# Third pair's increments and scores in one visit, the decay rows beside the spread of a, the second group's two pairs in one block, and no filler products: a Mamba-2 scan with a gated feed-forward block

## Chip, cores and metric

One core of a Trainium2 chip runs the whole kernel in one launch. The metric is the time on the device in microseconds (us), as the median over runs. The core has five engines that are used here: PE (TensorE, with its weight loads shown as PEld), DVE (VectorE), ACT (ScalarE), POOL (GpSimd) and SP, which only issues DMAs. Each engine works through its own queue strictly in the order of the program; between engines, semaphores hold an instruction back until what it needs is there.

## The reference

`batch, heads, seq, head_dim, d_state` are 4, 8, 768, 32, 16. The scan's result is turned to 3072 tokens of 256 values and goes through a feed-forward block with 2048 hidden values. All data are float32, the two weights come as float64.

```python
log_a = np.log(np.clip(a, 1e-06, 1.0))
for c in range(nc):                       # chunks of 32 in the reference
    cum = np.cumsum(la, axis=-1)
    L = np.exp(cum[:, :, :, None] - cum[:, :, None, :]) * causal
    M = np.einsum('bhin,bhjn->bhij', Cc, Bc) * L
    y_intra = np.einsum('bhij,bhjd->bhid', M, xc)
    y_inter = np.einsum('bhin,bhnd->bhid', Cc, state) * np.exp(cum)[:, :, :, None]
    y[:, :, sl] = y_intra + y_inter
    decay_from_j = np.exp(cum[:, :, -1:] - cum)
    Bx = np.einsum('bhjn,bhjd->bhjnd', Bc, xc) * decay_from_j[:, :, :, None, None]
    state = decay_full[:, :, None, None] * state + np.sum(Bx, axis=2)
...
h = x @ w_in                              # x: (3072, 256)
g = h * (1.0 / (1.0 + np.exp(-1.702 * h)))
return g @ w_out
```

## The kernel before, in words

The kernel uses chunks of 128 steps. A *pair* is two neighbouring chunks of all eight heads of one batch (12 pairs, numbered from 0), a *group* is two pairs, 512 tokens (6 groups, numbered from 0). The pairs that the title calls the second group's are pairs 6 and 7: they are turned while group 1, the second, is projected. While the feed-forward part of one group runs on PE, the scan of later groups is woven in between.

The scan of a pair has these steps. `turn_only` transposes B and C on PE into a PSUM tile `tp` (L491) and copies them out on ACT (BT and two CT, L496). `since_start` multiplies C by the decay since the start (CsT, DVE L524). `gain` makes the state's increments A (PE L567, 32-column strips of the array), `keep` turns them into states S on DVE (L582, L589). `score` makes C·B (tile cb, PE L539, 32-row strips), `weigh` multiplies them into the decay matrix L on DVE (L550). `finish` adds the two parts of y on PE (L603, L612) and copies yT out on ACT. `decay` makes the decay matrix of a chunk by a scan on DVE (L347) from rows of `a` that a DMA spread over the partitions, and `ends` scales B by its last column (L392). `clip_rows` and `decay_rows` make the decay since the start of a batch from another copy of `a`.

The opening is different. The decay of the first two pairs comes from logarithms: a cumulative sum on DVE (`cum`, L290), differences on PE (`differ`, L455, on top of a mask that `mask` has put there, L447) and exponentials on ACT (`exps`, L474). Before that, one product of ones (`keep_busy(1)`, L373) and two mask products into a tile that nobody reads (`idle`) run on PE. The weights arrive as two 32-bit words per value and are turned into float32 in ten pieces: `fields` (DVE L157, L160), `clamp` (ACT L168, L169), `rounded` (DVE L173), `join` (DVE L184, L190); `narrow(i)` is `rounded(i)`, `fields(i+1)`, `join(i)`. Pieces 0 to 5 are w_in, 6 to 9 are w_out.

Pair 2 is the third pair. Its decay is made on the chip without a DMA: `fan_all` spreads picked rows of `a` with four products in 32-row strips (L355) into an area of four PSUM banks, and four scans on DVE follow (L382). `since_fanned` makes the rest of batch 0's decay since the start: a spread of six chunks' rows by PE (`rows`, L422), a small one of the starts (`starts`, L436), a copy and a scan on DVE (L441, L442).

Group 0's feed-forward part is plain: `hidden(0, f)` for f from 0 to 15 (PE L654 into a bank `h`, Silu on ACT L657), then `project_all(0)` (PE L766 into two banks `o`), with steps of the scan hung into places of both by `at(in_hidden[0], f, ...)` and `at(in_project[0], f, ...)`. Group 1 has plain hidden products and a projection by seven products of mixed blocks (`product`, PE L823, with operands mixed on DVE by `mix_w`, L791, and `mix_g`, L694 to L696); its steps are H0 to H7 and P0 to P5, with work hung in by `at(after, step, ...)`. Groups 2 to 5 use seven products for the hidden part too (`first`, PE L726 and L736, with `mix_y` making the operands `my`), and the lists of steps in `run` fix the order on PE. In each of them, `ahead` is called two products into the sixth part of the projection: both pairs of a later group are transposed, gained, and kept there, with `mix_y` between.

PSUM: four banks of the pool `ps` (tag "ff") hold, in turn, all of tp, A, h, o, y, X, Y, rows and starts; four more are the area for cb, the spread of `a`, or the accumulators.

Of the kernel before, what the change touches and what calls it, by code (L numbers as in the profile page):

```python
# [16 lines left out]
P = 128  # L17
# [18 lines left out]
def kernel(  # L36
# [41 lines left out]
    NC = S // P  # L78
# [4 lines left out]
    CG = TG // P  # L83
# [79 lines left out]
    def clamp(i):  # L163


        e = power[i]
        z = e.bitcast(FP32)
        nc.scalar.activation(z, e, AF.Relu, scale=-8.0, bias=edge[:, 0:1])  # L168
        nc.scalar.activation(e, z, AF.Relu, scale=-1.0, bias=edge[:, 1:2])  # L169

    def rounded(i):

        nc.vector.scalar_tensor_tensor(out=mantissa[i].bitcast(FP32), in0=bits[i][0],  # L173
                                       scalar=2.0 ** -32, in1=mantissa[i],
                                       op0=ALU.mult, op1=ALU.add)
# [176 lines left out]
    def fan(p, r, ab):  # L352

        rows = slice(32 * r, 32 * r + 32)
        nc.tensor.matmul(out=ab, lhsT=ones[rows], rhs=fans[p][rows].rearrange("p k q i -> p (k q i)"),  # L355
                         start=True, stop=True, tile_position=(32 * r, 0),
                         skip_group_check=True)

    def fan_all(p):

        ab = area(f"ab{p}")
        for r in range(R):
            fan(p, r, ab[:, r])
        for r in range(R):
            decay_heads(p, r, ab[:, r])
        for k in range(2):
            ends(p, k)
# [51 lines left out]
    def fan_rows(t, c0, c1):  # L419

        o = bank(f"rows{c0}")[:, :(c1 - c0) * P]
        nc.tensor.matmul(out=o, lhsT=whose.rearrange("p h n -> p (h n)"),  # L422
                         rhs=t[:32, c0:c1].rearrange("p c s -> p (c s)"), start=True,
                         stop=True, tile_position=(0, 0), skip_group_check=True)
        return o
# [4 lines left out]
        nc.scalar.activation(since[0][:, :CG].rearrange("p c s -> p (c s)"),  # L430
                             fan_rows(cum, 0, CG), AF.Exp)

    def since_fanned():

        t, f = fan_rows(az, CG, NC), bank("starts")[:, :NC - CG]
        nc.tensor.matmul(out=f, lhsT=whose.rearrange("p h n -> p (h n)"),  # L436
                         rhs=starts[1][:32, CG:, 0], start=True, stop=True,
                         tile_position=(0, 0), skip_group_check=True)
        first = ssd.tile([P, NC, P], FP32, tag="first", name="first0", bufs=1)[:, CG:]
        nc.gpsimd.memset(first, 0.0)  # L440
        nc.vector.tensor_copy(first[:, :, 0], f)  # L441
        nc.vector.tensor_tensor_scan(  # L442
            out=since[0][:, CG:].rearrange("p c s -> p (c s)"), data0=t,
            data1=first.rearrange("p c s -> p (c s)"), initial=0.0, op0=ALU.mult, op1=ALU.add)

    def mask(t):
        nc.tensor.matmul(out=t, lhsT=identb, rhs=below.unsqueeze(1).to_broadcast([P, 4, P]),  # L447
                         start=True, stop=False, skip_group_check=True)
# [31 lines left out]
    def bank(name):  # L480
        return ps.tile([P, 4 * P], FP32, tag="ff", name=name)
# [71 lines left out]
    def advance(p):  # L553
        gain(p)
        keep(p)
# [374 lines left out]
    for r in range(2):  # L930
        ab[1, r] = bank(f"ab1_{r}")
        mask(ab[1, r])
    idle = bank("idle")
    for i in range(2):
        mask(idle)
    differ(0, [(r, ab[0, r]) for r in range(R)])
    exps(0, range(R))
    nc.vector.tensor_copy(idents, ident.unsqueeze(1).to_broadcast([P, NH, P]))
# [1 line left out]
    since_exp()  # L940
    fields(0)
    clamp(0)
    score(0, ab0)
    differ(1, [(r, ab[1, r]) for r in range(2)])
    exps(1, range(2))
# [1 line left out]
    ends(0, 0, nc.gpsimd)  # L947
    ends(0, 1, nc.gpsimd)
    weigh(0)
    rounded(0)  # L950
    turn_only(1, ("ACT", "ACT", "ACT"))
    gain(0)
    for r in range(2, R):
# [31 lines left out]
    def at(places, i, *work):  # L985
        places.setdefault(i, []).extend(work)
# [12 lines left out]
    at(in_hidden[0], 8, lambda: pick_a(PG))  # L999
    at(in_hidden[0], 9, lambda: clamp(6))  # L1000
    at(in_hidden[0], 9, lambda: fan_all(PG))
    at(in_hidden[0], 11, since_fanned, lambda: narrow(6))
    at(in_hidden[0], 15, lambda: clamp(7))
    for k in range(2):
        at(in_hidden[0], 5 + k, lambda k=k: spread(CG + 2 + k))
    at(in_hidden[0], 6, lambda: load(PG + 1))
    at(in_project[0], 0, lambda: turn_only(PG), lambda: narrow(7), lambda: since_start(PG))
    at(in_project[0], 1, lambda: advance(PG), lambda: clamp(8), lambda: decay(CG + 2))
    at(in_project[0], 4, lambda: scores(PG), lambda: narrow(8))
    at(in_project[0], 6, lambda: finish(PG), lambda: clamp(9), lambda: decay(CG + 3),  # L1010
       lambda: clip_rows(1), lambda: decay_rows(1))
    at(in_project[0], 7, lambda: turn(PG + 1))
# [9 lines left out]


    after = {}
    n, p = 2 * PG, 3 * PG

    def late(p):
        gain(p)
# [6 lines left out]
       lambda: turn(n + 1))  # L1035
    at(after, "H3", lambda: finish(n), lambda: load(p + 1), lambda: late(n + 1))
    at(after, "H4", lambda: finish(n + 1))
    for k, i in enumerate(("H4", "P0", "P2", "P5")):
        at(after, i, lambda k=k: mix_w(k))
    for j in range(NF // 2):  # L1040
        at(after, f"P{min(j - 1, 5)}" if j else "H4", lambda j=j: mix_g(1, j))
    for k in range(CG):
        at(after, f"P{k}", lambda k=k: decay(3 * CG + k))
        at(after, "H1" if k < 2 else "H3", lambda k=k: spread(3 * CG + k))
    at(after, "P3", lambda: clip_rows(2), lambda: decay_rows(2), lambda: turn(p))
    at(after, "P4", lambda: mix_y(2), lambda: advance(p), lambda: turn(p + 1))
    at(after, "P5", lambda: advance(p + 1))
    assert [b for b in range(NB) if 3 * CG <= b * NC < 4 * CG] == [2]


# [7 lines left out]
    project_all(0, in_project[0])  # L1058
    load(p)
    spread_rows(2)  # L1060
    for step in "H0 H1 H2 H3 H4 P0 H5 P1 H6 P2 H7 P3 P4 P5".split():
        j = int(step[1:])
        if step[0] == "H":
            hidden(1, 2 * j)
            hidden(1, 2 * j + 1)
        else:
            product(1, j)
        for do in after.get(step, []):
            do()
# [14 lines left out]

    def seven(g, j):
        return [(g, j, (i,)) for i in ORDER]

    for g in range(2, NG):
        n, p = (g + 1) * PG, (g + 2) * PG
        more, most = g + 1 < NG, g + 2 < NG  # L1090
        chunks = list(range((g + 2) * CG, (g + 3) * CG)) if most else []
        rows = [b for b in range(NB) if most and (g + 2) * CG <= b * NC < (g + 3) * CG]
        if most:
            load(p)
            for c in chunks[:2]:
                spread(c)
            for b in rows:
                spread_rows(b)
        run(g, "0.1 P P 0.6 P P 0.7 P 0.5 P 0.2 P 0.D", seven(g - 1, 6))
        run(g, "1.1 0.S P 0.4 P P 1.6 P 0.3 0.T M P P 1.7 P 1.5 1.2 1.D C", seven(g - 1, 7),  # L1100
            M=lambda: mix_g(g, 0), C=lambda: combine(g - 1))
        def along():
            for r in rows:
                clip_rows(r)
                decay_rows(r)

        def refill():
            if most:
                load(p + 1)
                for c in chunks[2:]:  # L1110
                    spread(c)

        if more:

            run(g, "2.1 1.S 1.4 1.3 2.6 2.5 2.2 2.7 1.T s1 2.D 2.S w1 give 2.4 3.1 2.3 3.5 2.T 3.6 "
                "s2 w2 y1 refill 3.7 3.2 3.D along 4.1 P P 3.4 P 3.S 4.6 P 3.3 4.5 3.T M1 P P y2 4.7 P 4.2 4.D M2",
                seven(g, 0), s1=lambda: score(n), w1=lambda: weigh(n), give=lambda: give(g - 1),
                s2=lambda: score(n + 1), w2=lambda: weigh(n + 1), y1=lambda: finish(n),
                refill=refill, along=along, y2=lambda: finish(n + 1), M1=lambda: mix_g(g, 1),
                M2=lambda: mix_g(g, 2))  # L1120
            if most:
                decay(chunks[0])
        else:
            run(g, "2.1 1.S 1.4 1.3 2.6 2.5 2.2 2.7 1.T 2.D 3.1 2.S 2.4 3.5 3.6 2.3 3.2 3.7 2.T 3.D M",
                M=lambda: mix_g(g, 1))
        for j in range(5 if more else 4, NF // 2):
            h = "{1}.1 {0}.S P {0}.4 P {1}.6 P {0}.3 P {1}.7 {0}.T P {1}.5 P {1}.2 P {1}.D M".format(j - 1, j)
            run(g, h, seven(g, j - 4), M=lambda: mix_g(g, j - 2))
            if most:
                decay(chunks[j - 4])  # L1130
        k = NF // 2 - 1
        run(g, f"P {k}.S P {k}.4 P P {k}.3 {k}.T P P P", seven(g, 4))
        if not more:
            give(g - 1)
            for j in range(k - 1, k + 1):
                mix_g(g, j)
            break
        mix_g(g, 6)

        def ahead():  # L1140
            if most:
                for k in (p, p + 1):
                    turn_only(k)
                for k in (p, p + 1):
                    gain(k)
                for k in (p, p + 1):
                    since_start(k)
            mix_y(g + 1)
            if most:
                for k in (p, p + 1):  # L1150
                    keep(k)

        run(g, "P P A P P P P P", seven(g, 5), A=ahead)
        mix_g(g, 7)
    end(NG - 1, 5)

# [31 lines left out]
```

## Time and profile before

| what | us |
|---|---|
| median of 5 runs (375.55 to 376.22) | 375.86 |
| the profiled execution's own time | 375.86 |
| its span, first to last instruction | 374.1 |
| PE busy | 367.0 |
| PE weight loads busy | 284.9 |
| DVE busy | 267.4 |
| ACT busy | 152.2 |
| POOL busy | 10.6 |

The time of a run is 1.76 us more than the span: what lies around the instructions. DVE is busy for 71% of the span on the average, but that average hides two parts: in the stretch from 24 to 88 us, DVE has work nearly throughout (15.57 of 16 us and 45.27 of 48 us), while from 143 us on it has 141.88 of 231 us. PE is busy nearly throughout from 24 us to the end.

A row of the timeline has the start, the length, the engine, the source line, the operation, what is written and read, the shape (stationary rows * columns, then moving), and how many records were merged. One float32 product is two records of PE. In brackets: how long the engine had been idle and what ended that.

### The profile page before, as it was taken

To read this page: it belongs to the slowest core of one execution; us is meant where nothing else is said; L and a number is where in the kernel's file an instruction comes from. 1 tells how busy PE (TensorE), PEld (TensorE's weight loads), DVE (VectorE), ACT (ScalarE), POOL (GpSimd) and SP (SyncE) were. 2 spreads that over 40 slices of the span, in tenths; PEclk is the share of its full clock that TensorE was granted. 3 is DMA by queue.
4 is the path that set the end of the run, shared out by engine and by line. 5 is a ranking of instruction groups with operands and counts; after the bars stand their busy time and mean duration, and the time that the engine had idled before them with its cause. 6 is when DMAs were issued, how large, how long until landed. Compare 5 with 4: busy or idle time off the path is not lost.

```text
span 374.1 us, 5767 instructions
## 1 busy us (share of the span) xinstructions
PE 367.0 (98%) x2280; PEld 284.9 (76%) x2280; DVE 267.4 (71%) x439; ACT 152.2 (41%) x337; POOL 10.6 (3%) x34
## 2 busy tenths in 40 slices
PE   8999999999999999999999999999999999999995
PEld 4674467886457588788888878888878888888884
DVE  4899999999879966777887665888574355544443
ACT  4678562402321132553423554333454331554330
POOL 4200000100000010000000000000000000000000
PEclk9999999999999999999999999999999999999999
DMA  9998699715856110086300063000010000000011
GB/s 151 229 328 143 212 238 144 212 42 102 194 131 124 58 42 0 2 156 126 112 3 1 0 123 105 0 2 0 0 58 2 0 3 1 0 2 0 0 58 56
DMA packets 85794, 29.56 MB, mean 79 GB/s; under 512 B 75720, under 2 KB 79240, under 8 KB 85768
## 3 DMA queue, kind: packets, MB, share of 16 engines
q1 hardware_dynamic: 83320, 28.81, 33.0%
q10 hardware_dynamic: 2448, 0.39, 0.6%
q8 instruction: 18, 0.29, 0.3%
q14 instruction: 8, 0.07, 0.1%
HBM read 25.95 MB, written 3.24 MB: 78 GB/s over the span
## 4 chain that ended last, share of the span: by engine, by line
PE 94%; DVE 3%; ACT 1%; issue 1%; DVEq 0%; ACTq 0%
PE acc L823 32%; PE X L726 15%; PE h L654 13%; PE Y L736 11%; PE o L766 8%; PE cb L539 3%; PE y L612 3%; PE y L603 2%; PE h L668 1%; PE tp L491 1%; DVE L L550 1%; PE oT L857 1%; PE A L567 1%; PE ab L447 1%; PE busy L373 1%
## 5 line engine op out<-in xcount | busy, mean ns | idle before, releaser
L823 PE MATMUL acc<-mg,mw 128*128 128x256 f32 x240 | 65.3, 379 | 0.0
L731 ACT ACTIVATE ac<-X 128x256 f32<-128x256 f32 x64 | 24.5, 383 | 68.9 <-PE X L726 68.9
L823 PEld LDWEIGHTS acc<-mg,mw 128*128 128x128 f32 x240 | 45.6, 190 | 6.2
L654 PE MATMUL h<-yT,w_in 128*128 128x512 f32 x112 | 50.0, 595 | 0.0
L840 DVE TENSOR_TENSOR gT<-Y,ac 128x512 f32<-128x512 f32 x32 | 22.1, 691 | 38.8 <-PE Y L736 35.7
L703 ACT ACTIVATE gT<-gT 128x512 f32<-128x512 f32 x64 | 33.3, 520 | 28.5 <-DVE gT L840 28.5
L823 PE MATMUL acc<-gT,w_out 128*128 128x256 f32 x160 | 43.8, 380 | 0.0
L347 DVE TENSOR_TENSOR_SCAN L<-a,idents 128x1024 f32<-128x1024 f32 x18 | 41.1, 2282 | 0.0
L726 PE MATMUL X<-my,mi 128*128 128x256 f32 x128 | 38.7, 384 | 0.0
L654 PEld LDWEIGHTS h<-yT,w_in 128*128 128x128 f32 x112 | 20.8, 190 | 23.4 <-issue 22.4
L823 PEld LDWEIGHTS acc<-gT,w_out 128*128 128x128 f32 x160 | 30.1, 190 | 5.4 <-issue 1.4
L840 DVE TENSOR_TENSOR gT<-Y,b 128x256 f32<-128x256 f32 x32 | 13.5, 421 | 28.0 <-PE Y L736 27.7
L657 ACT ACTIVATE gT<-h 128x512 f32<-128x512 f32 x28 | 16.6, 595 | 39.6 <-PE h L654 39.5
L550 DVE TENSOR_TENSOR L<-L,cb 128x2048 f32<-128x2048 f32 (+1 forms) x12 | 25.3, 2107 | 5.7 <-PE cb L539 5.5
L766 PE MATMUL o<-w_out,gT 128*128 128x256 f32 x128 | 29.3, 383 | 0.0
L694 DVE TENSOR_TENSOR mg<-gT 128x512 f32<-128x512 f32 x40 | 27.3, 683 | 1.9 <-ACT gT L703 1.9
L726 PEld LDWEIGHTS X<-my,mi 128*128 128x128 f32 x128 | 23.8, 190 | 4.2 <-issue 1.2
L766 PEld LDWEIGHTS o<-w_out,gT 128*128 128x128 f32 x128 | 23.8, 190 | 4.1 <-issue 0.7
L823 PE MATMUL acc<-gT,mw 128*128 128x256 f32 (+1 forms) x86 | 24.0, 368 | 0.4 <-DVE c L840 0.4
L823 PE MATMUL acc<-mg,w_out 128*128 128x256 f32 x80 | 23.5, 379 | 0.0
L634 ACT ACTIVATE yT<-y 128x256 f32<-128x256 f32 x22 | 7.2, 381 | 35.8 <-PE y L612 35.5
L736 PE MATMUL Y<-yT,mi 128*128 128x256 f32 x64 | 19.5, 386 | 0.0
(145 smaller groups left out, 541.3 us busy)
## 6 DMA issues: line engine op xcount, KB each, us to landing
a<-scratch SPq DMA_DIRECT2D x18, 512.0 KB, 5.1
bits<-in_moe_w_out_dram SPq DMA_DIRECT2D x4, 1024.0 KB, 7.5
x<-in_x_dram SPq DMA_DIRECT2D x24, 128.0 KB, 3.2
out_dram<-ob SPq DMA_DIRECT2D x11, 256.0 KB, 2.4
bits<-in_moe_w_in_dram SPq DMA_DIRECT2D x4, 512.0 KB, 5.5
bits<-in_moe_w_in_dram SPq DMA_DIRECT2D x2, 1024.0 KB, 8.9
b<-in_B_dram SPq DMA_DIRECT2D x24, 64.0 KB, 3.7
c<-in_C_dram SPq DMA_DIRECT2D x22, 64.0 KB, 2.5
```

The costliest lines, as they stand in the source:

```text
L347: nc.vector.tensor_tensor_scan(out=Ls[p][:, k].rearrange("p r q i -> p (r q i)"), data0=ra[n], data1=idents.rearrange("p h i -> p (h i)"), ...
L550: nc.vector.tensor_tensor(out=Lv[:, k], in0=Lv[:, k], in1=cb.rearrange("p r k e -> p k r e")[:, k], op=ALU.mult)
L654: nc.tensor.matmul(out=h, lhsT=w_in[:, k, f * P:(f + 1) * P], rhs=yT[g][:, k], start=(k == 0), stop=(k == NK - 1))
L657: nc.scalar.activation(gT[g, j][:, i], h, AF.Silu, scale=GELU_SCALE)
L694: nc.vector.tensor_tensor(out=t[:, 0:2], in0=B[:, :, 1], in1=B[:, 0], op=ALU.subtract)
L703: nc.scalar.activation(o, i, AF.Silu, scale=GELU_SCALE)
L726: nc.tensor.matmul(out=s["X"], lhsT=lhsT, rhs=rhs, start=i == "1", stop=i == "4", skip_group_check=True)
L731: nc.scalar.activation(copy, s["X"], AF.Copy)
L736: nc.tensor.matmul(out=o, lhsT=lhsT, rhs=rhs, start=s.pop("new", False), stop=i != "5", skip_group_check=True)
L766: nc.tensor.matmul(out=o[k // 2][:, k % 2], lhsT=gT[g, f // 2][:, f % 2, k * P:(k + 1) * P], rhs=w_out[:, f], start=(f == 0 and k % 2 == 0 ...
L823: nc.tensor.matmul(out=acc[g][0][i][:, cols], lhsT=lhsT, rhs=rhs[:, cols], start=(j == 0 and i in (0, 2, 5, 6)), stop=(j == NF // 2 - 1), ...
L840: nc.vector.tensor_tensor(out=o, in0=v, in1=w, op=ALU.add)
```

## The change

Five edits, four of which move work on PE:

- The two filler products into `idle` are gone, and with them that PSUM bank.
- `rounded(0)` on DVE goes from behind `weigh(0)` to before `score(0)`.
- `since_fanned` is cut in two: its two products (`rows`, `starts`) go into a new function `fan_since`, called inside `fan_all` directly behind the four products of the spread, two hidden tiles earlier on PE. Its DVE part is hung in behind `fan_all`; the order on DVE stays as it was.
- Pair 2's `gain` goes from step 1 of group 0's projection to step 2, and its `score` from step 4 to step 2, directly behind `gain`. `weigh` stays at step 4.
- Pairs 6 and 7 were turned, gained and kept one after the other at P3, P4 and P5 of group 1, with `mix_y(2)` at P4. Now P5 becomes a `run` with `ahead` two products in, as in the later groups; `ahead` has moved out of the loop to be called there too. `mix_w(3)` and `mix_g(1, 6)` go from P5 to P4, and `mix_g(1, 7)` goes behind the last product of P5.

The order of instructions on ACT, POOL and SP is the same in both kernels; no DMA is moved.

```diff
@@ fan_all
         for r in range(R):
             fan(p, r, ab[:, r])
+        fan_since()
         for r in range(R):
             decay_heads(p, r, ab[:, r])
...
-    def since_fanned():
-
-        t, f = fan_rows(az, CG, NC), bank("starts")[:, :NC - CG]
+    def fan_since():
+        t = fanned["rows"] = fan_rows(az, CG, NC)
+        f = fanned["starts"] = bank("starts")[:, :NC - CG]
         nc.tensor.matmul(out=f, lhsT=whose.rearrange("p h n -> p (h n)"),
                          rhs=starts[1][:32, CG:, 0], start=True, stop=True,
                          tile_position=(0, 0), skip_group_check=True)
+
+    fanned = {}
+
+    def since_fanned():
+
+        t, f = fanned["rows"], fanned["starts"]
         first = ssd.tile([P, NC, P], FP32, tag="first", name="first0", bufs=1)[:, CG:]
...
-    idle = bank("idle")
-    for i in range(2):
-        mask(idle)
     differ(0, [(r, ab[0, r]) for r in range(R)])
...
     clamp(0)
+    rounded(0)
     score(0, ab0)
...
     weigh(0)
-    rounded(0)
     turn_only(1, ("ACT", "ACT", "ACT"))
...
-    at(in_hidden[0], 11, since_fanned, lambda: narrow(6))
+    at(in_hidden[0], 9, since_fanned)
+    at(in_hidden[0], 11, lambda: narrow(6))
...
-    at(in_project[0], 1, lambda: advance(PG), lambda: clamp(8), lambda: decay(CG + 2))
-    at(in_project[0], 4, lambda: scores(PG), lambda: narrow(8))
+    at(in_project[0], 2, lambda: gain(PG), lambda: score(PG), lambda: keep(PG),
+       lambda: clamp(8), lambda: decay(CG + 2))
+    at(in_project[0], 4, lambda: weigh(PG), lambda: narrow(8))
...
-    for k, i in enumerate(("H4", "P0", "P2", "P5")):
+    for k, i in enumerate(("H4", "P0", "P2", "P4")):
         at(after, i, lambda k=k: mix_w(k))
     for j in range(NF // 2):
-        at(after, f"P{min(j - 1, 5)}" if j else "H4", lambda j=j: mix_g(1, j))
+        if j < 7:
+            at(after, f"P{min(j - 1, 4)}" if j else "H4", lambda j=j: mix_g(1, j))
...
-    at(after, "P3", lambda: clip_rows(2), lambda: decay_rows(2), lambda: turn(p))
-    at(after, "P4", lambda: mix_y(2), lambda: advance(p), lambda: turn(p + 1))
-    at(after, "P5", lambda: advance(p + 1))
+    at(after, "P3", lambda: clip_rows(2), lambda: decay_rows(2))
...
-    for step in "H0 H1 H2 H3 H4 P0 H5 P1 H6 P2 H7 P3 P4 P5".split():
+    for step in "H0 H1 H2 H3 H4 P0 H5 P1 H6 P2 H7 P3 P4".split():
...
+    def ahead(g, p=None):
+
+        pairs = (p, p + 1) if p else ()
+        for k in pairs:
+            turn_only(k)
+        for k in pairs:
+            gain(k)
+        for k in pairs:
+            since_start(k)
+        mix_y(g)
+        for k in pairs:
+            keep(k)
+
+    run(1, "P P A P P P P P", seven(1, 5), A=lambda: ahead(2, p))
+    mix_g(1, 7)
```

More of the change, by code (lines that the diff above doesn't have):

```diff
@@ L1006 @@
     at(in_hidden[0], 6, lambda: load(PG + 1))
+    n, p = 2 * PG, 3 * PG
     at(in_project[0], 0, lambda: turn_only(PG), lambda: narrow(7), lambda: since_start(PG))
-    at(in_project[0], 1, lambda: advance(PG), lambda: clamp(8), lambda: decay(CG + 2))
-    at(in_project[0], 4, lambda: scores(PG), lambda: narrow(8))
+    at(in_project[0], 2, lambda: gain(PG), lambda: score(PG), lambda: keep(PG),
+       lambda: clamp(8), lambda: decay(CG + 2))
+    at(in_project[0], 4, lambda: weigh(PG), lambda: narrow(8))
     at(in_project[0], 6, lambda: finish(PG), lambda: clamp(9), lambda: decay(CG + 3),
@@ L1024 @@
     after = {}
-    n, p = 2 * PG, 3 * PG
     def late(p):
@@ L1138 @@
         mix_g(g, 6)
[L1140 to L1153, printed above, removed]
+        run(g, "P P A P P P P P", seven(g, 5), A=lambda: ahead(g + 1, p if most else None))
         mix_g(g, 7)
```

## The prediction

> **What bounds the kernel now.** I read the page's busy shares first, then PE's waits, then PE's timeline around each edit, with DVE's and ACT's beside it.
>
> ```profile
> PE 367.0 (98%) x2280; PEld 284.9 (76%) x2280; DVE 267.4 (71%) x439; ACT 152.2 (41%) x337; POOL 10.6 (3%) x34
> ...
> PE ab L539 <- ACT L L474: 0.5, 1, 0.5
> PE h L668 <- DVE w_in L190: 0.4, 1, 0.4
> PE acc L823 <- DVE c L840: 0.4, 1, 0.4
> ```
>
> PE is the bound: 98% busy, and the listed waits come to 1.3 us after its start. So only three things can move the time: PE work taken away, a new wait of PE, and the opening, where PE still waits for others. The first of these is not products here but switches. Take the merged rows of the timeline:
>
> ```profile
> 39.45 1.14 PE L355 MATMUL ab<-X,ones 32*128 32x512 f32 x8
> 40.52 3.70 PE L654 MATMUL h<-yT,w_in 128*128 128x512 f32 x8
> 44.15 0.69 PE L422 MATMUL rows<-az,whose 32*128 32x256 f32 x2
> 44.68 0.28 PE L436 MATMUL starts<-starts,whose 32*128 32x2 f32 x2
> 44.89 7.13 PE L654 MATMUL h<-yT,w_in 128*128 128x512 f32 x16
> ...
> 87.20 3.60 PE L654 MATMUL h<-yT,w_in 128*128 128x512 f32 x8
> ```
>
> Eight h records between whole-array neighbours take 3.43 (from 87.20 to the transposes at 90.63), eight between two visits to strips 3.63 (40.52 to 44.15). So leaving the whole array costs 0.10 and coming back 0.10, whatever is done there. Three edits join visits. No edit moves a DMA, and the order on ACT, POOL and SP stays, so only the queues of PE and DVE are argued below. The same switch is seen at the other two places:
>
> ```profile
> 54.12 0.32 PE L567 MATMUL A<-x,Be 128*32 128x64 f32 x8
> 54.37 5.45 PE L766 MATMUL o<-w_out,gT 128*128 128x256 f32 x24
> 59.74 1.15 PE L539 MATMUL cb<-CT,BT 32*128 32x256 f32 x16
> ...
> 73.67 0.43 PE L567 MATMUL A<-x,Be 128*32 128x64 f32 x16
> 74.03 1.15 PE L539 MATMUL cb<-CT,BT 32*128 32x256 f32 x16
> ...
> 138.07 0.43 PE L567 MATMUL A<-x,Be 128*32 128x64 f32 x16
> 138.43 0.44 PE L491 MATMUL tp<-ident,b 128*128 128x128 f32 x2
> ...
> 142.04 0.43 PE L567 MATMUL A<-x,Be 128*32 128x64 f32 x16
> ...
> 196.84 0.54 PE L567 MATMUL A<-x,Be 128*32 128x64 f32 x24
> ```
>
> **Decay rows with the spread.** Now: 0.10 to leave h, 0.74 in strips (44.15 to 44.89), 0.11 to come back (the 16 h records take 6.97 against 2 x 3.43): 0.95. Directly behind the spread, in 32-row strips already and with the way back paid anyway: two rows records at 0.215 (the later pitch at 44.47 to 44.68) and 0.03 for starts: 0.46. Gain 0.49; if the rows still paid a switch of their own at both ends, 0.28. I take 0.45, as the strips are the same. Something is given back: rows and starts now hold two of the four "ff" banks through three hidden tiles, and h_13 takes the bank of starts, so it waits for the copy L441, with all of PE behind it. The DVE order is unchanged, so L441 still ends at 46.28; PE comes to h_13 at 40.52 + 0.46 + twelve h records at 0.429 + 0.10 = 46.23. Wait 0.05 to 0.10. h_14 waits for the scan L442, done at 47.01, a microsecond before PE. Next, group 0's first projection product needs w_out from L190, which ends at 51.72; PE comes at 52.29 - 0.40 = 51.89. Cover 0.17, so the whole edit cannot bring over 0.57. Sum: 0.40 (0.20 to 0.49).
>
> **Third pair's increments and scores.** Now: leave 0.10, A 0.25 (54.12 to 54.37), back and out again 0.19 (24 o records take 5.37 against 24 x 0.216 = 5.18), cb 1.08 (59.74 to 60.82), back 0.10: 1.72. Pair 3 does both in one visit: 0.10 + 0.36 + 1.08 + 0.10 = 1.64 with twice the A records; eight more A records cost 0.36 - 0.25 = 0.11, so 1.53. Gain 0.19 (bounds 0.10 and 0.29, one switch or three). The score comes 16 o records (3.46) earlier. It needs CT, which ACT ends at 55.88 (row at 55.05, 0.83), or 55.48 after the first gain, as ACT's work there follows the last Silu and so PE. PE reaches the score at 51.89 + 16 x 0.216 + 0.10 + 0.25 = 55.70. Cover 0.2; behind it all of PE would wait. DVE's order stays: CsT, `keep`, the scan L347, then `weigh`, which waited 0.1 for the score and no longer does; it now ends near 62.7, and `finish`, at 64.47 - 0.59 = 63.88, still comes over 1 us later.
>
> **Second group's pairs in one block.** Now, from 134.51: transposes 0.44, back and forth with 0.10 (14 acc records take 3.12, elsewhere 3.02), A 0.36, transposes 0.49, 0.10, A 0.36, back 0.11: 1.96. As in the later groups (195.88 to 196.84 for eight transposes with the way out, A 0.48 for 24 records and 0.11 for eight more, back 0.10): 1.65. Gain 0.31 (0.20 to 0.35). What could wait: DVE does `mix_w(3)`, `mix_g(1, 5)`, `mix_g(1, 6)` from 134.0 on, 4.5 us by their rows (1.46 + 2 x 1.52), done at 138.5. PE begins the transposes at 134.51 + 3.02 (P4) + 0.86 (two products) = 138.40. ACT's copies of one pair now end 1.75 after its transposes begin (136.26), the second pair's follow 1.05 later, at 141.2; then CsT 0.4 on DVE and two of `my`'s operations, 0.69 and 0.43: usable from 142.7. PE asks for it after transposes and A (1.65), five products (2.16), X (0.43) and two products (0.86), at 143.5. In group 2 the same step is asked 5.0 us after the transposes began, and there PE didn't wait; here 5.1 us. If it slipped, X and all that follows would wait by as much. The four "ff" banks are all held for a moment (two tp, two A); X needs the first tp's, free at 140.5, and comes at 142.1. `mix_g(1, 7)` ends about 146.6, before DVE's next step at 147.1.
>
> **No fillers, and `rounded(0)`.**
>
> ```profile
> 5.20 1.49 DVE L290 TENSOR_TENSOR_SCAN cum<-carry,cum 128x256 f32<-128x256 f32 x2 [0.48 <-ACT cum L285]
> ...
> 5.63 0.87 PE L447 MATMUL idle<-below,identb 128*128 128x512 bf16 x2
> 6.43 1.15 PE L455 MATMUL ab<-cum,pick 32*128 32x256 f32 x16
> ```
>
> The first of the two scans has told PE at 6.12 that `differ` may go; the second filler is in the way, and `differ` starts at 6.43. Other starts come 0.05 after their release (the score at 10.63, released 10.58), so without fillers 6.17: gain 0.26. From here to 24 us a chain passes it on: `differ`, the exponentials (8.51), score, the second `differ`, its exponentials (17.00), `ends` on DVE at 18.12, w_in at 23.65, h at 23.80. `rounded(0)`, 0.68, falls into DVE's 0.90 of idle time before `weigh(0)` at 11.99 and buys nothing itself, as `ends` waits for ACT; it gives DVE 0.6 of slack there. Without that idle time it would cost 0.68 on the path to w_in.
>
> But the array is slow at first: the two records of its first product (L373, float32, 512 columns) start 1.02 apart, h records of the same size later 0.429; the masks start 0.427 apart (3.50 to 6.06), two of the same at 14.38 only 0.28. The granted clock's first record is at 6.18, 4.97 us after PE's first product, all of them busy. Without fillers PE is busy for 4.43 us, then idle for 0.53. No row shows what that does. If the clock still comes at 6.18, gain 0.26. If not, `differ` runs at half speed: its eight steps of 0.216 cost 1.73 more, less 0.26 for the earlier start: 1.47 lost, or more if it lasts. I take the 0.26: of the 4.97 us that now precede the grant 4.43 stay busy, 89%, and the idle 0.55 at 10.08 did not slow what followed.
>
> The Trainium skill, "TensorE: Matmul & The Clock Gate", section "Why this matters for your kernels", asks to keep TensorE busy for 4 us or more without a break, and its Part 1 has a free-running window of 3413 ns. The rule's 4 us are met before the gap, the window that would end at 6.18 is not full; by the latter reading the clock would come at 9.59 and the sum would be a gain of 0.90 less 1.47, a loss of 0.57.
>
> **Sum.** 0.40 + 0.19 + 0.31 + 0.26 = 1.16 on a span of 374.1. The profiled execution's own time equals the median, 375.86, so 374.70. The likeliest case's own range, from the bounds: 374.4 to 375.3 (lowest 0.49 + 0.29 + 0.35 + 0.31 = 1.44, highest 0.20 + 0.10 + 0.20 + 0.10 = 0.60, with 0.10 where the clock comes a little later and 0.31 where `differ` also closes the gap to 6.12; rounded).
>
> **Rivals.** (1) *The clock comes late.* One mechanism, the gap at 5.64. For it: the fillers end just where `differ` starts. Against it: the 89%. If the clock comes as long after 6.17 as it now comes after 1.21, at 11.14, only `differ` is hit (the later products wait for ACT): 375.86 - 0.90 + 1.47 = 376.4. If it stays away until the increments end at 14.45, the score, the second `differ` and the transposes (3.8 us of PE) nearly double, some 2.5 more: 379. Slower than before once it costs over 0.90.
> (2) *DVE keeps the pace.* DVE is busy nearly throughout from 24 to 88 us, and the cover at 51.72 is 0.17, at CT 0.2. If DVE or ACT falls behind by 0.3 to 0.5, the first two gains go into a wait: 375.86 - 0.57 = 375.3. Against it: DVE and PE both move with the opening.
> (3) *The block comes too early for DVE.* `my` late by 0.5 more than its cover of 0.8 would leave 375.2; by 1.3 more, nothing is left of the change, 376.0. Against it: group 2's rows.
>
> **How the numbers follow.** Forecast 0.55, (1) 0.27, (2) 0.12, (3) 0.06. About 0.2%, 0.75 us, is what a measurement of this kernel can tell from no change. Faster than 375.11: 0.53 of the forecast, 0.04 of (2), 0.01 of (3): 0.58. Within: 0.02, 0.08, 0.05 of these and 0.09 of (1): 0.24. Slower than 376.61: 0.18 of (1), its longer forms. Range 374.3 to 376.6: the forecast, (2), (3), the short form of (1), and 0.1 below for the spread of a median.
>
> **What would show it.** After: `differ` at 6.17 with eight steps of 0.216, w_in at 23.4; rows directly behind the spread with h_13's wait below 0.1; no PE wait at the score or at `my`; one visit each. Steps of 0.43 in `differ` would prove (1). I'd be wrong by more if a wait appears in a later group, where nothing was changed.

## The result, and the profile after

The changed kernel takes 374.94 us in the median of 21 runs (374.73 to 375.30), beside 375.72 for the kernel before in the same comparison (41 runs, 375.53 to 376.38). The ratio is 0.9977, with the 95% interval 0.9971 to 0.9983: the median is 0.78 us lower. Its profiled execution took 375.30 us, the slowest of the 21, with a span of 373.6; that of before took 375.86 with 374.1. So the profiled pair differs by 0.56 only. That it shows 0.2 less than the medians do is itself a result, as will be seen.

The busy shares of the changed kernel, and PE's waits (what waited, for whom, us in total, times, the longest):

```profile
PE 366.1 (98%) x2278; PEld 285.2 (76%) x2278; DVE 267.8 (72%) x439; ACT 152.1 (41%) x337; POOL 10.8 (3%) x34
...
PE ab L546 <- ACT L L481: 0.6, 1, 0.6
PE h L675 <- DVE w_in L190: 0.4, 1, 0.4
PE acc L830 <- DVE c L847: 0.4, 1, 0.4
PE ab L462 <- DVE cum L290: 0.3, 1, 0.3
```

PE is busy for 0.9 less and remains the bound. The three waits of before, for L, w_in and c, are still there. One is new: `differ` (L462) now stands and waits for the cumulative sum, where the fillers were. Neither the third pair's score nor `my` is in the list.

PE's timeline of the changed kernel, at the rows, at the third pair, at the second group's block:

```profile
39.60 1.14 PE L355 MATMUL ab<-X,ones 32*128 32x512 f32 x8
40.56 0.59 PE L423 MATMUL rows<-az,whose 32*128 32x256 f32 x2
41.00 0.27 PE L437 MATMUL starts<-starts,whose 32*128 32x2 f32 x2
41.20 10.72 PE L661 MATMUL h<-yT,w_in 128*128 128x512 f32 x24
...
55.74 0.32 PE L574 MATMUL A<-x,Be 128*32 128x64 f32 x8
55.99 1.15 PE L546 MATMUL cb<-CT,BT 32*128 32x256 f32 x16
57.07 6.31 PE L773 MATMUL o<-w_out,gT 128*128 128x256 f32 x28
...
138.10 0.38 PE L498 MATMUL tp<-ident,b 128*128 128x128 f32 x2
138.32 0.38 PE L498 MATMUL tp<-ident,c 128*128 128x128 f32 x2
138.54 0.38 PE L498 MATMUL tp<-ident,b 128*128 128x128 f32 x2
138.76 0.38 PE L498 MATMUL tp<-ident,c 128*128 128x128 f32 x2
139.07 0.65 PE L574 MATMUL A<-x,Be 128*32 128x64 f32 x32
139.65 0.70 PE L830 MATMUL acc<-gT,mw 128*128 128x256 f32 x2
```

Each of the three places has one visit to the strips now: the rows start 0.41 behind the start of the spread's last record, with no return in between; A and cb follow each other; the eight transposes are followed by all 32 records of A. But the 24 records of h behind the rows last 10.72, where 23 steps of 0.429, one length of 0.59 and 0.10 for coming back make 10.56: 0.16 has gone somewhere. And the opening is slower than before:

```profile
3.11 2.73 PE L454 MATMUL ab<-below,identb 128*128 128x512 bf16 x6
6.10 1.63 PE L462 MATMUL ab<-cum,pick 32*128 32x256 f32 x16 [0.26 <-DVE cum L290]
7.56 1.04 PE L462 MATMUL ab<-minus,cum 32*128 32x256 f32 x16
```

`differ` does start 0.33 earlier than before (6.43), yet its first half takes 1.63 instead of 1.15, so the second half begins at 7.56, later than before's 7.40. A trace also holds records of the clock that was granted to TensorE, each with its start and length. The first of them, at full clock, starts at 7.12 here and at 6.18 before. Ahead of 7.12 the steps of `differ` last 0.59 and 0.43, behind it 0.22.

Comparing the starts of the same PE records in the two traces, step by step, gives: opening +0.16; rows -0.41, then +0.15 given back among the hidden records before 47.1; third pair -0.20; second group's block -0.29; nothing at any later group. The sum is -0.59, beside -0.56 in the spans. `my`, which the prediction feared for, is ready in time: the two of its operations on DVE that the prediction names end at 142.37, and PE's first product with it starts at 143.21.

### The profile page after: what moved, and what is told of

It reads as the page before. It is cut to its first block, busy times and chain, and to the rows that moved or that the text cites. A ratio compares the mean times of both kernels' runs of the same rounds, so it can differ in the third digit from the quotient of the medians.

```text
span 373.6 us, 5764 instructions
## 1 busy us (share of the span) xinstructions
PE 366.1 (98%) x2278; PEld 285.2 (76%) x2278; DVE 267.8 (72%) x439; ACT 152.1 (41%) x337; POOL 10.8 (3%) x34
## 4 chain that ended last, share of the span: by engine, by line
PE 94%; DVE 2%; ACT 1%; DMA 1%; issue 0%; ACTq 0%; DVEq 0%
PE acc L830 32%; PE X L733 15%; PE h L661 13%; PE Y L743 11%; PE o L773 8%; PE cb L546 3%; PE y L619 3%; PE y L610 2%; PE ab L462 2%; PE h L675 1%; PE tp L498 1%; PE oT L864 1%; ACT L L481 1%; PE A L574 1%; DMA az<-in_a_dram 1%; DVE L L557 1%
## 5 line engine op out<-in xcount | busy, mean ns | idle before, releaser
L743 PE MATMUL Y<-yT,mi 128*128 128x256 f32 x64 | 19.5, 386 | 0.0
```

Source lines behind the costliest of these rows:

```text
L743: nc.tensor.matmul(out=o, lhsT=lhsT, rhs=rhs, start=s.pop("new", False), stop=i != "5", skip_group_check=True)
```

## The experiments

All times below are medians with the number of runs, and ratios are against runs of the kernel before, made beside them on the same chip. The recorded ratio is not the quotient of the two medians, so both are given. The kernels were measured in four groups, each with the kernel before beside it: the changed kernel (after) alone; the four with one part each (no_fill to block_only); early_copy with after_fill2, after_nobusy and after_late_rounded; after_again with early_copy_again and early_both. The mean of the kernel before was 375.82, 375.95, 375.93 and 375.82 in these groups, so a difference of 0.1 between kernels of two groups says nothing until each is set against its own before. Since the opening turned out to differ from execution to execution, the table also gives, from each profiled execution, the first record of the granted clock, the start of `differ`, the start of the first product of `h` from `y` ("h", near 19.5; the opening is what lies before it), and the time from there to the start of PE's last product. This last column has nothing of the opening in it: over the five executions that differ from the changed kernel in the opening at most it stays within 349.40 to 349.41, while h lies anywhere from 19.23 to 20.41.

| kernel | clock granted | differ | h | h to last product | lowest | median |
|---|---|---|---|---|---|---|
| before | 6.18 | 6.43 | 19.55 | 350.14 | 375.53 | 375.72 |
| no_fill | 4.41 | 6.09 | 19.21 | 350.15 | 375.55 | 375.74 |
| rows_only | 4.12 | 6.09 | 19.21 | 349.89 | 375.27 | 375.29 |
| third_only | 6.21 | 6.45 | 19.56 | 349.95 | 375.35 | 375.57 |
| block_only | 4.67 | 6.19 | 19.30 | 349.86 | 375.25 | 375.46 |
| after | 7.12 | 6.10 | 19.71 | 349.40 | 374.73 | 374.94 |
| after_again | 4.09 | 6.11 | 19.23 | 349.41 | 374.80 | 374.83 |
| after_fill2 | 6.90 | 6.62 | 19.86 | 349.41 | 374.81 | 375.43 |
| after_nobusy | 8.56 | 6.09 | 20.41 | 349.41 | 374.80 | 375.48 |
| after_late_rounded | 6.29 | 6.22 | 19.35 | 349.41 | 374.82 | 375.01 |
| early_copy | 6.76 | 6.09 | 19.52 | 349.29 | 374.66 | 374.72 |
| early_copy_again | 4.73 | 6.11 | 19.23 | 349.30 | 374.71 | 374.85 |
| early_both | 6.88 | 6.11 | 19.59 | 349.30 | 374.66 | 374.76 |

**One part at a time.** Four kernels have one edit each on top of the kernel before.

no_fill:

```diff
-    idle = bank("idle")
-    for i in range(2):
-        mask(idle)
```

> The kernel before without the two filler products of the opening, nothing else. Theory: differ can start some 0.26 to 0.33 us earlier, but the grant of the full clock comes at its own moment, which differs from execution to execution; what the first products gain is lost again when they run at half speed up to the grant. Median 0.00 to 0.26 below before, some 0.12 (375.6 beside 375.72); the profile's first product of differ near 6.1 and w_in between 23.4 and 23.9, depending on where the grant falls. Rival 1 (the fillers cost their own time and nothing else): 0.26 below, 375.46. Rival 2 (the fillers are what keeps the array busy enough for the grant, so the clock comes later without them): level to 0.6 above, 375.7 to 376.3.

Measured: 375.74 (12 runs) beside 375.83 (35), ratio 0.9992 (0.9984 to 1.0001). That is 0.09 in the median and 0.15 in the mean, near the theory's average of 0.12, but the ratio's centre fits rival 1's 0.26 (a ratio of 0.9993) better, and the interval holds no gain at all as well. So the times do not decide between the two. What speaks against rival 1 are the lowest times, which are level (375.55 and 375.54): in some executions the fillers cost nothing. Rival 2's loss of up to 0.6 would be a ratio of up to 1.0016, and all of it above 0.04 lies outside the interval. In the profiled execution the clock was granted at 4.41, before the place where the fillers were.

rows_only:

```diff
             fan(p, r, ab[:, r])
+        fan_since()
...
-    at(in_hidden[0], 11, since_fanned, lambda: narrow(6))
+    at(in_hidden[0], 9, since_fanned)
+    at(in_hidden[0], 11, lambda: narrow(6))
```

> The kernel before with the decay rows taken together with the spread of a, nothing else. Theory: 0.41 gross at the rows, and 0.15 given back at h_13, which waits 0.05 for the first copy of the starts and loses 0.10 more on restarting: 0.26 below before, 375.46. Rival 1 (what was predicted: a wait below 0.1 and no more): 0.35 to 0.40 below, 375.35. Rival 2 (VectorE sets the pace behind it, so the shift is lost at the first scores): within 0.10 of before.

Measured: 375.29 (12 runs) beside 375.83, ratio 0.9983 (0.9975 to 0.9992). The median fits rival 1 or more. The trace says otherwise: h to the last product is 0.25 shorter, and the lowest time is 0.27 below before's, as the theory has it. The rest of the median's 0.54 must then lie in the opening, which the edit does not touch; seven of the twelve runs lie between 375.27 and 375.29, and the profiled one of these (375.27) had its clock early, at 4.12.

third_only:

```diff
-    at(in_project[0], 1, lambda: advance(PG), lambda: clamp(8), lambda: decay(CG + 2))
-    at(in_project[0], 4, lambda: scores(PG), lambda: narrow(8))
+    at(in_project[0], 2, lambda: gain(PG), lambda: score(PG), lambda: keep(PG),
+       lambda: clamp(8), lambda: decay(CG + 2))
+    at(in_project[0], 4, lambda: weigh(PG), lambda: narrow(8))
```

> The kernel before with the third pair's increment and score products issued together, nothing else. Theory: one change of product shape is saved both ways, 0.20 below before, 375.52, with no wait of TensorE at that score. Rival (the score now waits for its masked operands, or the increment's later end delays VectorE): 0.00 to 0.10 below, and the wait is to be seen at the score.

Measured: 375.57 (11 runs) beside 375.83, ratio 0.9991 (0.9983 to 1.0000); lowest 0.19 lower, h to the last product 0.19 shorter. The interval holds the theory's 0.20 and the rival's 0.00 to 0.10; the trace decides. PE's timeline of third_only has no gap in front of the scores:

```profile
52.30 3.62 PE L766 MATMUL o<-w_out,gT 128*128 128x256 f32 x16
55.85 0.32 PE L567 MATMUL A<-x,Be 128*32 128x64 f32 x8
56.10 1.15 PE L539 MATMUL cb<-CT,BT 32*128 32x256 f32 x16
57.18 7.17 PE L766 MATMUL o<-w_out,gT 128*128 128x256 f32 x32
```

block_only is the second group's part alone (the lists of `at` and `run` for group 1, and `ahead` outside the loop):

```diff
-    at(after, "P3", lambda: clip_rows(2), lambda: decay_rows(2), lambda: turn(p))
-    at(after, "P4", lambda: mix_y(2), lambda: advance(p), lambda: turn(p + 1))
-    at(after, "P5", lambda: advance(p + 1))
+    at(after, "P3", lambda: clip_rows(2), lambda: decay_rows(2))
...
+    run(1, "P P A P P P P P", seven(1, 5), A=lambda: ahead(2, p))
+    mix_g(1, 7)
```

> The kernel before with the second group's two pairs turned in one block, nothing else. Theory: 0.29 to 0.31 below before, 375.42, with no wait at my. Rival (my's copy comes too late once the block is moved, since the rows' earlier end is not there to help): a wait of 0.1 to 0.8 at my or at the second pair's output, 0.2 below to 0.5 above before.

Measured: 375.46 (12 runs) beside 375.83, ratio 0.9986 (0.9977 to 0.9994); lowest 0.29 lower, h to the last product 0.28 shorter. PE's list of waits shows nothing at `my`.

The three parts together: 0.25 + 0.19 + 0.28 = 0.72 from h to the last product, where the changed kernel has 350.14 - 349.40 = 0.74. They add up, so none of the three hides another.

**The opening.** PE's timeline of after_again, which is the changed kernel itself in another execution, and of rows_only, which still has the fillers:

```profile
3.12 1.92 PE L454 MATMUL ab<-below,identb 128*128 128x512 bf16 x6
6.11 1.15 PE L462 MATMUL ab<-cum,pick 32*128 32x256 f32 x16 [1.07 <-DVE cum L290]
7.08 1.05 PE L462 MATMUL ab<-minus,cum 32*128 32x256 f32 x16
```

```profile
3.11 1.94 PE L454 MATMUL ab<-below,identb 128*128 128x512 bf16 x6
4.89 0.59 PE L454 MATMUL idle<-below,identb 128*128 128x512 bf16 x2
6.09 1.15 PE L462 MATMUL ab<-cum,pick 32*128 32x256 f32 x16 [0.61 <-DVE cum L290]
```

The six masks take 1.92 and 1.94 here and 2.73 in the profiled executions of before and after: the clock came during them, at 4.09 and 4.12. Then the fillers are through at 5.5, `differ` waits for the cumulative sum all the same, and starts at 6.11 without them and at 6.09 with them. So in these executions the fillers cost nothing. What they cost where the clock comes late, after_fill2 shows:

```diff
+    idle = bank("idle")
+    for i in range(2):
+        mask(idle)
     differ(0, [(r, ab[0, r]) for r in range(R)])
```

> The changed kernel with the two filler products put back, nothing else. Theory: executions in which the clock is granted early (below 4.7) cost nothing more, those in which it comes late cost 0.17 to 0.33; lowest time within 0.05 of the changed kernel's 374.73, mean some 0.12 above its 374.95. Rival 1 (the fillers cost their own time always): 0.26 above in lowest and mean. Rival 2 (the fillers keep the array busy for the grant): level or faster, by up to 0.4.

Measured: 375.43 (11 runs) beside 375.90 (33), ratio 0.9981 (0.9973 to 0.9990); lowest 374.81. The lowest time speaks for the theory against rival 1, at 0.08 rather than within 0.05. The mean is 0.29 above that of the changed kernel, but 0.10 of this stands between the two groups' means of the kernel before; the other 0.19, with standard errors of 0.09 and 0.04 for the two kernels, lies between the theory's 0.12 and rival 1's 0.26 and tells neither from the other. Its profiled execution is a late one:

```profile
3.11 2.73 PE L454 MATMUL ab<-below,identb 128*128 128x512 bf16 x6
5.63 1.06 PE L454 MATMUL idle<-below,identb 128*128 128x512 bf16 x2
6.62 1.25 PE L462 MATMUL ab<-cum,pick 32*128 32x256 f32 x16
```

With the clock at 6.90, the fillers run at half speed to the end and `differ` starts at 6.62, not 6.43; h begins at 19.86, while early_both, without fillers and with the clock at 6.88, has it at 19.59. In this one pair of late executions, then, the fillers cost 0.27. That is about half of the 0.51 by which `differ` starts later, as it should be if the part of `differ` that could have run in that time would have run at half speed. In early executions they cost nothing that can be seen: rows_only with fillers has h at 19.21, no_fill and after_again without them at 19.21 and 19.23. In block_only, with fillers, h comes at 19.30, but there too `differ` waited for the cumulative sum, which itself came late. How often an early or a late clock occurs is not settled by these few executions.

What sets the clock's moment? after_nobusy leaves out the product of ones, two records on PE (its bank is still taken, so that the other tiles come in the same banks):

```diff
-    keep_busy(1)
+    bank("busy")
```

> The changed kernel without the warming products that run from 1.2 to 3.1, so that TensorE's first product is the one at 3.1; the output stays the same. Theory (the full clock is granted at the end of a window of 3.413 of which the array was busy for most, with a phase that nobody sets): the first grant lies between 6 and 9.5 instead of between 4 and 7.2, so the median is 0.5 to 1.2 above the changed kernel, and the executions spread more widely. Rival (the grant comes at a fixed delay from the first product, some 3 to 4): a spread no wider than now, all executions slower by about 1.0. Third case (the phase alone decides, whatever the array did): level with the changed kernel.

Measured: 375.48 (11 runs, 374.80 to 376.17) beside 375.90, ratio 0.9988 (0.9979 to 0.9996). The spread is 1.37 instead of 0.57, the clock came at 8.56 in the profiled execution, and the fastest execution is as fast as the changed kernel. The median is 0.54 above the changed kernel's, which is at the theory's lower edge; against the kernel before of each group it is 0.36. In kind this is the theory. A fixed delay from the first product would not have widened the spread, and the changed kernel itself speaks against one: its clock came 2.88 us after PE's first product in after_again and 5.92 after it in after. Against the third case, that the phase alone decides, stands that the clock did not come one window earlier, at 8.56 - 3.41 = 5.15, though PE had been at work for the last 2.04 of the 3.41 us ahead of it (60%); the intervals of the two ratios overlap a little, so the times alone do not rule it out. PE in that execution:

```profile
3.11 2.72 PE L454 MATMUL ab<-below,identb 128*128 128x512 bf16 x6 [3.11 <-POOL below L273]
6.09 2.09 PE L462 MATMUL ab<-cum,pick 32*128 32x256 f32 x16 [0.27 <-DVE cum L290]
```

The first half of `differ` starts at about the same moment as in after_again (6.11) and takes 2.09 instead of 1.15.

after_late_rounded puts `rounded(0)` back:

```diff
-    rounded(0)
     score(0, ab0)
...
     weigh(0)
+    rounded(0)
```

> The changed kernel with the rounding of the first pair's operands back behind the first weigh, nothing else. Theory (its move was hidden in VectorE's idle time ahead of the weigh, and nothing waits for it there): within 0.06 of the changed kernel in mean and in lowest time. Rival (the move brought part of the gain that is put down to the other parts): slower by 0.1 to 0.3.

Measured: 375.01 (9 runs) beside 375.90, ratio 0.9978 (0.9968 to 0.9987): 0.07 above the changed kernel in the median, 0.10 in the mean (standard errors 0.06 and 0.035), 0.09 in the lowest. Taken so, that is above the theory's 0.06 and at the edge of the rival's 0.1. But the kernel before of this group also has a mean 0.10 higher; against their own before the two means are level (0.87 below it each), as are the ratios, 0.9978 and 0.9977. Its trace has h at 19.35 with `differ` at 6.22 (here the cumulative sum came later), so 13.13 between them; after_again has 13.12. So nothing of the move is to be seen on the path.

**The stall behind the rows.** early_copy is the changed kernel with the copy of the starts ahead of the four scans of the spread on DVE:

```diff
         fan_since()
+        first_since()
         for r in range(R):
             decay_heads(p, r, ab[:, r])
...
-    def since_fanned():
-
-        t, f = fanned["rows"], fanned["starts"]
+    def first_since():
         first = ssd.tile([P, NC, P], FP32, tag="first", name="first0", bufs=1)[:, CG:]
+        fanned["first"] = first
         nc.gpsimd.memset(first, 0.0)
-        nc.vector.tensor_copy(first[:, :, 0], f)
+        nc.vector.tensor_copy(first[:, :, 0], fanned["starts"])
+
+    def since_fanned():
+
+        t, first = fanned["rows"], fanned["first"]
         nc.vector.tensor_tensor_scan(
```

> The changed kernel with the first copy of the starts issued ahead of the four scans of the spread instead of behind them, so that the bank of the starts is free before h_13 asks for it. Theory (the 0.15 given back at h_13 is that wait of 0.05 and a restart of 0.10, both gone with the wait): no wait of TensorE at h_13, 0.15 below the changed kernel, 374.8 beside 374.95. Rival 1 (the 0.10 behind the wait belongs to h after the rows, whatever waits): 0.05 below. Rival 2 (VectorE's scans end 0.15 to 0.19 later and the next wait takes it all): level with the changed kernel or slower by up to 0.1.

Measured: 374.72 (12 runs, 374.66 to 375.15 and one at 376.76), ratio 0.9975 (0.9964 to 0.9985). The median is 0.22 below that of the changed kernel, which belongs to another group; the ratios differ by 0.0002 only, and h to the last product is 0.11 shorter. So it was measured again with the changed kernel beside it on the same chip, and with a third kernel, early_both, that also sets the ones for the warming product first:

> The changed kernel itself once more, beside the two that follow on one chip. Every theory: 374.95 in the median, within 0.15; lowest 374.73 to 374.80.

> The version with the early first copy once more, beside the changed kernel on the same chip. Theory (0.16 won back at h_13, in every execution): mean and lowest 0.10 to 0.20 below the changed kernel's of this call. Rival (the earlier difference came from the moment of the grant in those executions): lowest within 0.05 of the changed kernel's.

```diff
+    ones = const.tile([P, P], FP32, name="ones")
+    nc.vector.memset(ones, 1.0)
     early = const.tile([P, 1], FP32, name="early")
     nc.vector.memset(early, 1.0)
...
-    ones = const.tile([P, P], FP32, name="ones")
-    nc.vector.memset(ones, 1.0)
```

> The version with the early first copy, and the ones for the warming products set first on VectorE instead of fourth, so that TensorE starts some 0.1 earlier. Theory (the grant comes at the end of a window in which the array was busy long enough, so its latest moment moves earlier by as much as the start): the latest executions gain 0.05, the earliest nothing, mean 0.01 to 0.05 below the version with the early copy, which this measurement can hardly tell from nothing. Rival (the grant comes at a fixed delay from the first product): every execution whose grant falls after 6.1 gains 0.05, no early ones exist. Third case (what is put behind the ones on VectorE, and ScalarE's table behind it, is late): slower by 0.1 or more.

Measured, with before at 375.75 (19 runs): after_again 374.83 (9 runs, 0.9973, interval 0.9964 to 0.9983), early_copy_again 374.85 (8 runs, 0.9975, 0.9965 to 0.9985), early_both 374.76 (8 runs, 0.9975, 0.9965 to 0.9985). Lowest 374.80, 374.71 and 374.66; means 374.89, 374.88, 374.88. The expected 0.10 to 0.20 is missed in the mean (level, with standard errors of 0.04 and 0.06), and the lowest, 0.09, lies between theory and rival. The traces settle the mechanism all the same. The same seven hidden records of group 0 in after_again and then in early_copy_again:

```profile
44.69 3.32 PE L661 MATMUL h<-yT,w_in 128*128 128x512 f32 x7
```

```profile
44.69 3.17 PE L665 MATMUL h<-yT,w_in 128*128 128x512 f32 x7
```

They start at the same moment and take 0.15 less without the wait. On DVE the copy of after ends in front of the long scan; in early_copy_again it comes 5 us sooner. DVE of after, then of early_copy_again:

```profile
46.29 0.15 DVE L448 COPY first<-starts 128x2 f32<-128x2 f32 x1
46.48 0.69 DVE L449 TENSOR_TENSOR_SCAN since<-rows,first 128x256 f32<-128x256 f32 x1
```

```profile
40.90 0.16 DVE L448 COPY first<-starts 128x2 f32<-128x2 f32 x1
40.98 4.56 DVE L384 TENSOR_TENSOR_SCAN L<-ab,idents 128x512 f32<-128x512 f32 x4
```

In the profiled execution of after, the copy releases its bank at 46.46 and h_13 (the first product of group 0's hidden tile 13) starts at 46.50, 0.05 late; its second record comes 0.533 behind the first instead of 0.429. The weight load of h_13 names what it waited for:

```profile
46.50 0.30 PEld L661 LDWEIGHTS h<-yT,w_in 128*128 128x128 f32 x2 [0.71 <-DVE first L448]
```

In early_copy both the wait and the longer step are gone, so the 0.10 belongs to the wait and not to the rows: rival 1 of early_copy is out. Of the 0.15, 0.03 to 0.04 are lost again at group 0's first projection record (the second one comes 0.253 behind it instead of 0.218). DVE's row for w_out ends 0.18 before PE comes there, instead of 0.30 in after_again, which makes w_out the likely cause; no wait is listed there, so this is not shown. What remains to the end is 0.11. The scatter of a mean of eight executions, 0.06, is too large to show it well. early_both starts its first product 0.09 earlier and shows no loss; a gain of the size expected of it, 0.01 to 0.05, cannot be told from nothing here.

## Why the prediction was right, and where it was not

The forecast case came true in the main: but for 0.15 at h_13, no wait took the place of the switches, and the median came to 374.94 where 374.70 was predicted. Part of that closeness is luck. The forecast gain was 1.16 and the measured one is 0.78; the predicted time is off by 0.24 and not by 0.38 because it started from a median of five runs, 375.86, and over 41 runs the kernel before has 375.72. By the steps:

- *Third pair, 0.19:* 0.20 in the profiled pair, 0.19 alone. Leaving and coming back once less, worked from the length of eight records between different neighbours, was the right price. The cover of 0.2 at CT held: the copy on ACT ends at 55.78, the score starts at 55.99.
- *Second group's block, 0.31:* 0.29, and 0.28 alone. `my` was not waited for; its cover was 0.84 where 0.8 was predicted, so rival (3) did not occur.
- *Decay rows with the spread, 0.40:* 0.25 to 0.26. The mechanism was right and two terms were mis-sized. The gross gain was 0.41 instead of 0.45: behind the spread, `rows` and `starts` put h off by 0.53 (from the spread's last record begun to h, 1.05 instead of 0.52), not by the 0.46 that was priced. And the wait at h_13 was foreseen with its place and its size (0.05 to 0.10; it was 0.05), but it was taken at its own length; the record behind it comes 0.10 later as well, so 0.15 goes. The step's range of 0.20 to 0.49 held the result.
- *No fillers, 0.26:* this is the step that failed. "If the clock still comes at 6.18, gain 0.26" took the clock's moment in one profiled execution for a property of the kernel. It lay anywhere from 4.09 to 7.12 in the profiled executions of kernels with the same first products. Without fillers `differ` did start near 6.10, even before the predicted 6.17, in all of them but after_late_rounded (6.22). What that brings was 0.27 in the pair of executions with a late clock and nothing to be seen in those with an early one, and no_fill alone showed 0.09 in the median. In the profiled pair the opening shows a loss of 0.16, with after's clock 0.94 later than before's. That chance accounts for the spans' 0.56 beside the medians' 0.78.
- *`rounded(0)` for nothing:* its move cannot be seen on the path.
- *Rival (1), the clock comes late:* after's own profile, read alone, would seem to prove it, since the first steps of `differ` run at 0.59 and 0.43. The prediction named steps of 0.43 as the proof. They are none: after_again, the same program, got its clock at 4.09, and its first half of `differ` takes the same 1.15 as before's; after_late_rounded got its clock at 6.29, with the whole gap of 0.38 in the 3.41 us ahead of it. So the gap at the fillers' place did not keep the clock away.
- *Rival (2), DVE keeps the pace:* not in the change itself. In early_copy_again, where PE came 0.15 earlier still, 0.03 to 0.04 were lost at the first product with w_out, though w_out's row had ended 0.18 before it. If that is w_out's doing, a cover read from the rows, such as the prediction's 0.17 there, cannot be used up in full.
- *The rule of the Trainium skill* ("TensorE: Matmul & The Clock Gate", Part 1 and "Why this matters for your kernels"): a free-running window of 3413 ns, and 4 us or more of TensorE busy without a break. On the window the runs agree: the granted stretch is 368.639 or 365.226 us long in every trace (365.225 in two), 108 or 107 times 3.4133. The prediction read from the page that a window which is not full gives no clock, and estimated 9.59. The traces say that not so much is needed, nor 4 us: in after_again the clock came 2.88 us after PE's first product. In after, a window ended at 7.12 - 3.41 = 3.71 and gave nothing; the array had worked from 1.20 on, 2.51 of 3.41 us, 74%. In after_again the one that ended at 4.09 held 2.88 (from 1.21), 84%, and gave the clock. If the busy share of a window decides, the limit lies between these two; no run varied that share alone.

So of the 1.16 predicted, the three visits saved brought 0.74 (predicted 0.90). The rest is the opening (predicted 0.26), with the chance of the clock in it on both sides: 0.04 by the medians, 0.13 by the means, which differ by 0.87, and 0.19 by the means of after_again and its before.

## What to carry to other kernels

Where TensorE is busy 98% of the time, as here, products that leave the whole array for strips are worth putting together: each of the three edits brought 0.19 to 0.28 us net, and the parts added up. When a moved product holds a buffer for longer, ask who releases it, and price a stall at its length plus the restart behind it (0.05 and 0.10 at h_13). Before a difference of some tenths between two profiled executions is put down to an edit, look at what differs between executions of one program: here the moment of the granted clock went with a shift of 0.48 in the opening, more than the largest single edit brought (0.28), while the time from a fixed record behind the opening to the last one, the same to 0.01 in five executions, gave each edit from a single profile.

## What was not expected of the hardware

- The full clock of one program came at moments 3 us apart in two executions (4.09 and 7.12). With it, the first product of h from `y` moved from 19.23 to 19.71, though `differ` started at the same time in both.
- A product that had waited 0.05 for its bank was followed by its second record 0.10 later than usual (0.533 for 0.429 between two records of 512 columns). The same 0.533 stands behind a return from the strips (44.89 to 45.42 in the kernel before), so the short stall cost as much behind it as a return does.
- Without the warming products the fastest execution (374.80) is as fast as with them (374.73 and 374.80); in these runs they narrowed the spread (0.57 and 0.33, against 1.37) rather than lowered the best time.
